# A retention layer into a gated product on one core: where block 1's first product stands, and which engine converts the weights

## The chip, the cores and the metric

The kernel runs on one core of a Trainium2 chip. The metric is the device time of one execution in microseconds. Before the change three runs gave 781.29, 781.69 and 781.89 us, median 781.69.

Engines by the profile's names: PE multiplies matrices (PEld is its load of the stationary operand), DVE is the vector engine, ACT the scalar engine, POOL is GpSimd, and SP's queue (SPq) issues nearly all loads. Times inside the execution are counted from the first instruction.

## The reference, cut to what matters

For each of 4 batches and 8 heads a recurrence runs over 768 steps, and its output, 3072 rows of 512, goes through two matrix products with a sigmoid gate between them.

```
state = gamma * state + outer(k[t], v[t]);   y[t] = scale * q[t] @ state      # head_dim 64
x = y as (4*768, 8*64) = (3072, 512)
h = x @ w_in                    # w_in  512 x 2048
g = h * sigmoid(1.702 * h)
out = g @ w_out                 # w_out 2048 x 512
```

w_in and w_out reach the kernel as 64-bit floats (8 bytes for each weight), and the kernel turns them into 32-bit floats on the chip.

## The kernel before, in words

**Blocks and chunks.** The 3072 rows are six blocks of 512 rows, and a block is four chunks of 128 steps. One chunk j of the recurrence is three steps: `turn(j)` transposes q and k (on PE for chunks 0 to 7, L194, evacuated by ACT, L195; on DVE later, L197) and makes the decayed k on POOL (`kd`, L201); `attend(j)` multiplies k by q on PE (`pa`, L210) and masks it with two DVE multiplications (`at`, L213); `finish(j)` adds the state's part (L223) and the chunk's own part (L227) into `py`, DVE scales that into X (L230), and PE makes the state's update `pu` (L237), which POOL (L244) and DVE (L246, or L242 in the first chunk of a batch) add to the state.

**The two products of a block.** Block 0 takes plain products: `up0(f)` makes the f-th of 16 tiles of h, 128 rows by 512, with four matmuls (L260); ACT takes the sigmoid (L252) and DVE multiplies it in (L253) into G. `down0(f)` adds tile f's part of the output with four matmuls (L272) into four accumulators in PSUM. Both need only the converted weights. Blocks 1 to 5 take `up(d)` and `down(m)`, which make seven products of half size in place of eight (L312, L363). They need sums of the weights, which `sums_w1` and `sums_w2` make on POOL (L281 to L284, L288 to L291), and sums of X and G.

**The weights.** They come in 32 pieces of 512 KB, each a tile of 128 by 512 weights as pairs of 32-bit words (`lo`, `hi`); pieces 0 to 15 are w_in and 16 to 31 w_out. `fetch` loads a piece into one of three raw buffers, which lie in W2's slots 4 to 6. `narrow` converts one piece with eight operations that follow on each other, through two sets of three scratch tiles: ACT takes the magnitude of `hi` (L171); POOL clamps it (L172); DVE shifts it (L173), puts the sign back (L174) and takes the exponent out (L175); ACT converts and scales `lo` (L176); POOL multiplies it by the exponent (L177); DVE adds the two into W1 or W2 (L180). Then the next piece is fetched. Tile f of h needs pieces up to f + 1 at most; `down0(f)` needs piece 16 + f.

**What sets the order.** PE runs in the order that the code is written in. The orders of DVE, ACT, POOL and of SP's queue are made by a scheduler from the same program. Every engine takes its instructions strictly in its order. The code's order is: chunks 0 to 3 with two pieces converted in each; `up0` of block 0, one piece with each tile; `down0` of block 0, one piece with each f, with chunks 4 to 7 and `sums_w1` between them; then blocks 1 to 5, each `up`, then `down` with the next block's chunks between.

The tiles of h go through four PSUM buffers (two tags of two), which are also the four accumulators of `down0`: PE can be four tiles of h ahead of DVE's multiplication.

Of the kernel before, what the change touches and what calls it, by code (L numbers as in the profile page):

```python
# [9 lines left out]
F32 = mybir.dt.float32  # L10
# [18 lines left out]
def kernel(  # L29
# [25 lines left out]


    nc = tc.nc
    pe, act, dve, pool, sp = nc.tensor, nc.scalar, nc.vector, nc.gpsimd, nc.sync
# [32 lines left out]
    G = const.tile([P, NP, 4, TH], F32, name="G")  # L91
    rowd = const.tile([P, HP, P], F32, name="rowd")
    cold = const.tile([P, 2 * H + HP], F32, name="cold")
# [6 lines left out]

    def load(j):

# [8 lines left out]
        if j < 2 * CB:  # L111
            plain("q", q, "q_sq", 2)
            plain("kn", k, "k_sq", 2)
        else:
            for name, src in (("q", q), ("k", k)):
                t = two.tile([P, HP, P // C4, C4], F32, name=name + "_sq")
                for r0 in range(0, P, C4):
                    d0 = r0 % D
                    for hp in range(HP):
                        sp.dma_start(t[r0:r0 + C4, hp],  # L120
                                     src[b, 2 * hp + r0 // D, rows, d0:d0 + C4].rearrange("(s p) d -> p s d", p=C4))
                QKV[name, j] = t
            if c < NC - 1:
                plain("kn", k, "kn", 1)
        plain("v", v, "v", 2)
# [4 lines left out]
    stage = W2[:, 4:7].rearrange("p s n e -> p (s n e)")  # L130
    NRAW, NTMP = 3, 2
    RAWS = [stage[:, 1024 * i:1024 * (i + 1)].bitcast(U32).rearrange("p (n two) -> p n two", two=2)
            for i in range(NRAW)]
    TMPS = [[stage[:, 1024 * NRAW + 512 * (3 * i + t):1024 * NRAW + 512 * (3 * i + t + 1)] for t in range(3)]
            for i in range(NTMP)]

    PIECES = []
    for p in range(NP):
        for h in range(2):
            dst = W1[:, p, 0:4:3] if h == 0 else W1[:, p, 1:3]  # L140
            PIECES.append((dst.rearrange("p ab c f -> p c ab f"), w1v[:, 2 * h:2 * h + 2, 2 * p * P:2 * (p + 1) * P]))
    for p in range(NP):
        for ab in range(2):
            PIECES.append((W2[:, 0:4:3, p] if ab == 0 else W2[:, 1:3, p], w2v[:, 2 * p + ab]))
    N1 = 2 * NP
# [12 lines left out]
    def narrow(n=1):  # L158


        for _ in range(n):
            i = narrowed[0]
            if i == len(PIECES):
                return
            narrowed[0] = i + 1
            w, x = PIECES[i][0], RAWS[i % NRAW]
            lo, hi = x[:, :, 0], x[:, :, 1]
            m, e, r = TMPS[i % NTMP]
            mu, eu = m.bitcast(U32), e.bitcast(U32)

            act.activation(m, hi.bitcast(F32), AF.Abs, scale=2.0 ** 16)  # L171
            pool.tensor_scalar(m, m, F64_MOST * 2.0 ** 16, F64_LEAST * 2.0 ** 16, op0=ALU.min, op1=ALU.max)  # L172
            dve.tensor_scalar(mu, mu, 3, None, op0=ALU.logical_shift_left)  # L173
            dve.scalar_tensor_tensor(mu, hi, 0x80000000, mu, op0=ALU.bitwise_and, op1=ALU.bitwise_or)  # L174
            dve.tensor_scalar(eu, mu, 0xFF800000, None, op0=ALU.bitwise_and)  # L175
            act.activation(r, lo, AF.Copy, scale=2.0 ** -52)  # L176
            pool.tensor_mul(r, r, e)  # L177
            shape = "p (c ab f) -> p c ab f" if i < N1 else "p (s e) -> p s e"
            sizes = dict(c=2, ab=2) if i < N1 else dict(s=2)
            dve.tensor_add(w, m.rearrange(shape, **sizes), r.rearrange(shape, **sizes))  # L180
            fetch()


    QT, KT, KD, AT = {}, {}, {}, {}

    def turn(j):

        for name, store in (("q", QT), ("k", KT)):
            t = one.tile([P, HP, P], F32, name=name + "T")
            if j < 2 * CB:  # L190
# [8 lines left out]
        if j % NC < NC - 1:  # L199
            KD[j] = one.tile([P, H, D], F32, name="kd")  # L200
            pool.tensor_mul(KD[j], QKV.pop(("kn", j)), cold[:, H:2 * H, None].to_broadcast([P, H, D]))  # L201
        if CB <= j < NCH and (j % CB < 2 or j < 2 * CB - 1):
            load(j + (2 if j >= 2 * CB else 1))

    def attend(j):
        p = ps_a.tile([P, 2, HP, P], F32, name="pa")
        for hp in range(HP):
            for i in range(2):
                r = slice(i * D, (i + 1) * D)
                pe.matmul(p[:, i, hp, :], KT[j][r, hp, :], QT[j][r, hp, :], start=True, stop=True)  # L210
        AT[j] = one.tile([P, 2, HP, P], F32, name="at")
        for i in range(2):
# [3 lines left out]
    def finish(j):  # L216
# [12 lines left out]
        half, t0 = divmod(j % CB * P, TH)  # L229
        dve.tensor_mul(X[:, 2 * half:2 * half + 2, :, t0:t0 + P].rearrange("p s c t -> p (s c) t"), y, rowd)  # L230
        if c == NC - 1:
# [17 lines left out]
    def hidden(g, h):  # L249

        s = two.tile([P, 2, TH], F32, name="sg")
        act.activation(s, h, AF.Sigmoid, scale=1.702)  # L252
        dve.tensor_mul(g, h, s)  # L253

    def up0(f):
        p, ab = divmod(f, 2)
        h = ps.tile([P, 2, TH], F32, name="ph", tag="xy"[f % 2])
        for c in range(4):
            w = W1[:, p, (c // 2 if ab == 0 else (3, 2)[c // 2]), c % 2, :]
            pe.matmul(h, w, X[:, c // 2:4:2, c % 2, :], start=(c == 0), stop=(c == 3))  # L260
        hidden(G[:, p, ab:4:2, :], h)

    PO = {}

    def down0(f):
        p, ab = divmod(f, 2)
        for n in range(CB):
# [3 lines left out]
            w = W2[:, 0:4:3, p, :] if ab == 0 else W2[:, 1:3, p, :]  # L271
            pe.matmul(PO[n], G[:, p, 2 * half + ab, t0:t0 + P], w, start=(f == 0), stop=(f == NFF - 1))  # L272
            if f == NFF - 1:
# [130 lines left out]
    load(1)  # L404
    fetch()
    fetch()
    make_identity(nc, ident)
# [11 lines left out]

    for j in range(CB):  # L420
        if j + 2 <= CB:
            load(j + 2)
        turn(j)
        attend(j)
        narrow(1)
        finish(j)
        narrow(1)
    for f in range(NFF):
        up0(f)
        narrow(1)  # L430
    narrow(1)

    def chunks(m):
# [3 lines left out]

    between = chunks(1)
    for f in range(NFF):
        down0(f)  # L440
        narrow(1)
        if between and f >= 2:
            between.pop(0)()
        if f % 4 == 3:
            sums_w1(f // 2 - 1)
    sums_x()
    for m in range(1, NB):
        for d in range(NP // 2):
            up(d)
            if m == 1:  # L450
                sums_w2(2 * d)
            if m + 1 < NB and d < 2:
                load((m + 1) * CB + d)
        between = chunks(m + 1) if m + 1 < NB else []
        for n, unit in enumerate(down(m)):
            unit()
            if between and n % 2:
                between.pop(0)()
# [48 lines left out]
```

## Time and profile before

| what | value |
|---|---|
| median of three runs | 781.69 us |
| the profiled execution's own time, and its span | 782.11 us, 780.3 us |
| PE busy, of the span | 725.1 us, 93% |
| DVE busy | 368.6 us, 47% |
| POOL busy | 206.3 us, 26% |
| ACT busy | 153.4 us, 20% |
| moved by DMA | 46.27 MB, mean 59 GB/s |

The page cuts the span in 40 slices of 19.5 us and gives each engine's busy share in tenths. PE's row reads 4679677499999999999999999999999999999998: the first eight slices, some 156 us, are the only ones in which PE is not nearly always busy. DVE's row begins 3678868761 and POOL's 2776665584 in the same slices. A busy share is an average over a slice. Which wait ended last has to be read from the rows of the chain and the timeline.

### The profile page before, as it was taken

How to read it: one execution, taken by the hardware profiler on the slowest of the kernel's cores; microseconds unless marked ns; L12 is line 12 of the kernel's file. 1: busy time of each engine (PE TensorE's matmuls, PEld its weight loads, DVE VectorE, ACT ScalarE, POOL GpSimd, SP SyncE). 2: the span in 40 equal slices, each digit the busy share in tenths (PEclk: the TensorE clock that was granted, in tenths of full speed). 3: DMA queues.
4: the chain of work that ended last, by engine and by line, in shares of the span. 5: the costliest groups of instructions: out<-in, count | busy, mean ns of one | idle time of the engine just before them, and what ended most of it. 6: DMA issues, size and time to landing. Idle time of an engine off the chain costs nothing.

```text
span 780.3 us, 9581 instructions
## 1 busy us (share of the span) xinstructions
PE 725.1 (93%) x3648; PEld 572.4 (73%) x3648; DVE 368.6 (47%) x547; ACT 153.4 (20%) x253; POOL 206.3 (26%) x195
## 2 busy tenths in 40 slices
PE   4679677499999999999999999999999999999998
PEld 3454222155568888888888888888888888888886
DVE  3678868761144336334436434445334364244251
ACT  3233334310103310013300023300033200033100
POOL 2776665584140004020014220012300022200030
PEclk9879878699999999999999999999999999999999
DMA  8634323312241003340022331022430030100001
GB/s 202 185 113 149 134 108 109 133 29 55 45 109 23 1 15 77 56 99 14 1 54 53 84 60 22 1 50 55 85 71 1 0 69 13 42 1 1 1 13 41
DMA packets 142253, 46.27 MB, mean 59 GB/s; under 512 B 129920, under 2 KB 135552, under 8 KB 142208
## 3 DMA queue, kind: packets, MB, share of 16 engines
q1 hardware_dynamic: 135504, 39.10, 21.5%
q10 hardware_dynamic: 6704, 6.57, 2.5%
q8 instruction: 29, 0.48, 0.2%
q14 instruction: 16, 0.13, 0.1%
HBM read 39.33 MB, written 6.29 MB: 58 GB/s over the span
## 4 chain that ended last, share of the span: by engine, by line
PE 77%; DVE 11%; POOL 7%; issue 3%; DMA 1%; SPq 0%; ACT 0%; POOLq 0%; DVEq 0%
PE pd L363 30%; PE px L312 18%; PE py L312 13%; PE po L272 5%; PE py L227 4%; POOL W L177 3%; PE pu L237 3%; PE pa L210 3%; DVE W L174 3%; DVE W L180 2%; DVE W L173 2%; PE py L223 2%; DVE W L175 1%; POOL W L172 1%; DMA W<-in_moe_w_in_dram 1%
## 5 line engine op out<-in xcount | busy, mean ns | idle before, releaser
L363 PE MATMUL pd<-W,G 128*128 128x256 f32 x1120 | 250.3, 381 | 0.4 <-DVE G L303 0.3
L363 PEld LDWEIGHTS pd<-W,G 128*128 128x128 f32 x1120 | 210.1, 190 | 30.8 <-DVE G L303 1.2
L312 PE MATMUL px<-X,W 128*128 128x256 f32 x640 | 148.7, 379 | 0.0
L312 PEld LDWEIGHTS px<-X,W 128*128 128x128 f32 x640 | 121.6, 190 | 17.0 <-issue 0.5
L312 PE MATMUL py<-X,W 128*128 128x256 f32 x480 | 113.4, 379 | 0.0
L312 PEld LDWEIGHTS py<-X,W 128*128 128x128 f32 x480 | 91.2, 190 | 12.4
L201 POOL TENSOR_TENSOR kd<-kn_in,cold 128x512 f32<-128x512 f32 x20 | 22.2, 1110 | 294.3 <-PE pu L237 200.4
L260 PE MATMUL ph<-X,W 128*128 128x512 f32 x128 | 65.8, 671 | 16.9 <-DVE G L253 16.9
L272 PE MATMUL po<-W,G 128*128 128x512 f32 x128 | 61.8, 628 | 10.4 <-DVE G L253 10.4
L213 DVE TENSOR_TENSOR at<-pa,mask 128x512 f32<-128x512 f32 x48 | 30.9, 685 | 83.6 <-PE pa L210 83.5
L260 PEld LDWEIGHTS ph<-X,W 128*128 128x128 f32 x128 | 26.6, 214 | 55.4 <-issue 30.9
L304 POOL TENSOR_TENSOR G<-G 128x512 f32<-128x512 f32 x20 | 29.0, 1449 | 111.5 <-DVE G L303 107.0
L272 PEld LDWEIGHTS po<-W,G 128*128 128x128 f32 x128 | 24.3, 199 | 39.2 <-issue 24.9
L252 ACT ACTIVATE sg<-G 128x512 f32<-128x512 f32 x60 | 37.8, 631 | 64.0 <-DVE G L322 38.3
L177 POOL TENSOR_TENSOR W<-W 128x512 f32<-128x512 f32 x32 | 43.5, 1360 | 25.8 <-DVE W L175 25.8
L253 DVE TENSOR_TENSOR G<-G,sg 128x512 f32<-128x512 f32 x60 | 41.3, 689 | 17.4 <-ACT sg L252 17.4
L227 PE MATMUL py<-at,v_in 128*64 128x128 f32 x384 | 32.2, 303 | 11.3 <-DVE at L213 11.3
L180 DVE TENSOR_TENSOR W<-W 128x512 f32<-128x512 f32 x32 | 30.3, 946 | 26.4 <-POOL W L177 26.1
L171 ACT ACTIVATE W<-W 128x512 f32<-128x512 f32 x32 | 21.6, 675 | 87.7 <-DVE W L180 79.1
L227 PEld LDWEIGHTS py<-at,v_in 128*64 128x64 f32 x384 | 24.5, 150 | 17.1 <-DVE at L213 13.7
L210 PEld LDWEIGHTS pa<-qT,kT 64*128 64x128 f32 x384 | 24.1, 193 | 15.4 <-issue 7.3
L322 DVE TENSOR_TENSOR G<-py,p 128x512 f32<-128x512 f32 x20 | 13.8, 692 | 44.4 <-PE py L312 44.4
(66 smaller groups left out, 620.5 us busy)
## 6 DMA issues: line engine op xcount, KB each, us to landing
W<-in_moe_w_in_dram SPq DMA_DIRECT2D x16, 512.0 KB, 4.0
W<-in_moe_w_out_dram SPq DMA_DIRECT2D x16, 512.0 KB, 3.2
v_in<-in_v_dram SPq DMA_DIRECT2D x24, 256.0 KB, 3.3
out_dram<-o ACTq DMA_DIRECT2D x24, 256.0 KB, 2.3
kn_in<-in_k_dram SPq DMA_DIRECT2D x21, 256.0 KB, 3.7
q_sq<-in_q_dram SPq DMA_DIRECT2D x256, 16.0 KB, 1.8
k_sq<-in_k_dram SPq DMA_DIRECT2D x256, 16.0 KB, 1.7
q_in<-in_q_dram SPq DMA_DIRECT2D x8, 256.0 KB, 5.2
```

Source lines behind the costliest of these rows:

```text
L177: pool.tensor_mul(r, r, e)
L180: dve.tensor_add(w, m.rearrange(shape, **sizes), r.rearrange(shape, **sizes))
L210: pe.matmul(p[:, i, hp, :], KT[j][r, hp, :], QT[j][r, hp, :], start=True, stop=True)
L213: dve.tensor_mul(AT[j][:, i], p[:, i], mask[:, i])
L227: pe.matmul(y[i * D:(i + 1) * D, hp, :], vn[:, 2 * hp + i, :], a[:, i, hp, :], start=(not c and hp == 0), stop=(hp == HP - 1), skip_group_ ...
L252: act.activation(s, h, AF.Sigmoid, scale=1.702)
L253: dve.tensor_mul(g, h, s)
L260: pe.matmul(h, w, X[:, c // 2:4:2, c % 2, :], start=(c == 0), stop=(c == 3))
L272: pe.matmul(PO[n], G[:, p, 2 * half + ab, t0:t0 + P], w, start=(f == 0), stop=(f == NFF - 1))
L304: pool.tensor_sub(g[1], g[1], g[0])
L312: pe.matmul(acc[:, u, :], W1[:, 2 * d + u, sa, c, :], X[:, sb, c, :], start=(start and u == 0 and c == 0), stop=(stop and c == 1), skip_gr ...
L363: pe.matmul(p0[:, n, :], G[:, p, sa, n * P:(n + 1) * P], W2[:, sb, p, :], start=(new and p == 0 and n == 0), stop=(last and p == NP - 1), ...
```

## The change

Three things move together.

**The order.** Chunks 4 to 7 run between the tiles of `up0` of block 0 (one step after each tile from the third on), block 1 then takes its first product in the plain form too (`up0(1, f)`, 16 tiles in place of four `up(d)`), and only then comes `down0` of block 0. In the first four chunks `turn(j + 1)` now stands between `attend(j)` and `finish(j)`. `sums_w2` stands in `down0`, `sums_w1` in block 1's `down`.

**The conversion.** After ACT's magnitude, all six operations on a piece are DVE's: clamp, shift, sign, exponent, product, sum. They are done in place, in the raw buffer and in the piece's own place in W1 or W2, so that no scratch tiles are left. ACT converts `lo` no more and POOL does nothing for a piece. There are four raw buffers in place of three, in slots 4 and 5 of W2.

**Where things lie.** Block 0's G goes to slots 4 to 6 of W1, slots 4 to 6 of X and a small tile, since block 1's takes the old place; its DVE multiplications are cut in two halves of 256. Block 1's X lies in slot 6 of W2. For chunks 0 to 7 the transposed q, k, the decayed k and the masked product lie in G, in two sets.

```diff
-    NRAW, NTMP = 3, 2
+    NRAW = 4
...
             act.activation(m, hi.bitcast(F32), AF.Abs, scale=2.0 ** 16)
-            pool.tensor_scalar(m, m, F64_MOST * 2.0 ** 16, F64_LEAST * 2.0 ** 16, op0=ALU.min, op1=ALU.max)
+            dve.tensor_scalar(m, m, F64_MOST * 2.0 ** 16, F64_LEAST * 2.0 ** 16, op0=ALU.min, op1=ALU.max)
             dve.tensor_scalar(mu, mu, 3, None, op0=ALU.logical_shift_left)
-            dve.scalar_tensor_tensor(mu, hi, 0x80000000, mu, op0=ALU.bitwise_and, op1=ALU.bitwise_or)
-            dve.tensor_scalar(eu, mu, 0xFF800000, None, op0=ALU.bitwise_and)
-            act.activation(r, lo, AF.Copy, scale=2.0 ** -52)
-            pool.tensor_mul(r, r, e)
...
-            dve.tensor_add(w, m.rearrange(shape, **sizes), r.rearrange(shape, **sizes))
+            dve.scalar_tensor_tensor(hi, hi, 0x80000000, mu, op0=ALU.bitwise_and, op1=ALU.bitwise_or)
+            dve.tensor_scalar(mu, hi, 0xFF800000, None, op0=ALU.bitwise_and)
+            r = lo.bitcast(F32)
+            dve.scalar_tensor_tensor(r, lo, 2.0 ** -52, m, op0=ALU.mult, op1=ALU.mult)
...
+                dve.tensor_add(w, xf[:, :, :, :, 1], xf[:, :, :, :, 0])
...
+        for g, h, s in [(g, h, s)] if not isinstance(g, list) else [(g[i], h[:, i], s[:, i]) for i in range(2)]:
+            dve.tensor_mul(g, h, s)
...
+    def g0(p, s):
+        if s < 3:
+            return W1[:, p, 4 + s].rearrange("p c f -> p (c f)")
+        return X[:, 4 + p // 2, p % 2] if p < 6 else G0[:, p % 2]
...
+    turn(0)
     for j in range(CB):
-        if j + 2 <= CB:
-            load(j + 2)
-        turn(j)
         attend(j)
         narrow(1)
+        turn(j + 1)
         finish(j)
         narrow(1)
+    between = chunks(1)[1:]
     for f in range(NFF):
-        up0(f)
+        up0(0, f)
+        if f < NP or f % 4 == 3:
+            narrow(1)
+        if between and f >= 2:
+            between.pop(0)()
+    for f in range(NFF):
+        up0(1, f)
         narrow(1)
-    narrow(1)
...
     for f in range(NFF):
         down0(f)
-        narrow(1)
-        if between and f >= 2:
-            between.pop(0)()
         if f % 4 == 3:
-            sums_w1(f // 2 - 1)
-    sums_x()
+            sums_w2(f // 2 - 1)
```

How the orders move, at the two places on which the prediction rests. First PE, from block 0's first product on, before (`ph` is a tile of h, `po` block 0's output, `pt`, `pa`, `py`, `pu` the steps of a chunk):

```order
L260 MATMUL ph<-X,W_72 128x512 x64
L272 MATMUL po<-W_73,G 128x512 x12
L194 MATMUL pt<-ident,q_in 128x128 x4
L194 MATMUL pt<-ident,kn_in 128x128 x4
L272 MATMUL po<-W_73,G 128x512 x4
L210 MATMUL pa<-qT,kT 128x128 x8
L272 MATMUL po<-W_73,G 128x512 x4
```

And now, from chunk 7's masked product on (X1 lies in W2, hence `ph<-W_73`; block 0's G lies in W1 and X):

```order
L231 MATMUL pa<-G 128x128 x8
L291 MATMUL ph<-X,W_72 128x512 x4
L244 MATMUL py<-G,state_82 128x128 x4
L248 MATMUL py<-G,v_in 64x128 x8
L261 MATMUL pu<-v_in,G 128x128 x4
L291 MATMUL ph<-X,W_72 128x512 x12
L291 MATMUL ph<-W_73,W_72 128x512 x64
L303 MATMUL po<-W_73,W_72 128x512 x6
```

The chunks now stand among the tiles of `ph`, and sixteen more tiles stand ahead of the first `po`.

Second DVE, while pieces of w_out are converted. Before (L253 is the multiplication into G):

```order
L174 SCALAR_TENSOR_TENSOR W_73<-W_73 128x512
L175 TENSOR_SCALAR W_73<-W_73 128x512
L173 TENSOR_SCALAR W_73<-W_73 128x512
L174 SCALAR_TENSOR_TENSOR W_73<-W_73 128x512
L253 TENSOR_TENSOR G<-ph,sg 128x2x256
L180 TENSOR_TENSOR W_73<-W_73 128x2x256
L175 TENSOR_SCALAR W_73<-W_73 128x512
L180 TENSOR_TENSOR W_73<-W_73 128x2x256
```

And now, in block 1's first product (L178 clamp, L179 shift, L180 sign, L181 exponent, L183 product, L190 sum, L278 the multiplication into G):

```order
L180 SCALAR_TENSOR_TENSOR W_73<-W_73 128x512 [waits DMAHW1_49,DVE_49]
L278 TENSOR_TENSOR W_72<-ph,sg 128x256 [waits Activation_49]
L278 TENSOR_TENSOR g_76<-ph,sg 128x256
L181 TENSOR_SCALAR W_73<-W_73 128x2x256 [waits DVE_49]
L178 TENSOR_SCALAR W_73<-W_73 128x2x256
L183 SCALAR_TENSOR_TENSOR W_73<-W_73 128x512 [waits DVE_49]
L179 TENSOR_SCALAR W_73<-W_73 128x2x256 [waits DVE_49]
L190 TENSOR_TENSOR W_73<-W_73 128x2x256 [waits DVE_49]
L180 SCALAR_TENSOR_TENSOR W_73<-W_73 128x512 [waits DMAHW4_49,DVE_49]
L278 TENSOR_TENSOR G<-ph,sg 128x2x256 [waits Activation_49]
```

Two pieces are woven into each other, so that an operation seldom stands right behind the one that it waits for, and none of DVE's rows waits for POOL. In DVE's whole order the last piece's sum stands ahead of the multiplication of tile 6 of block 1: 32 halves and 6 whole multiplications stand ahead of it, and tiles 6 to 15 behind.

More of the change, by code (lines that the diff above doesn't have):

```diff
@@ L91 @@
     G = const.tile([P, NP, 4, TH], F32, name="G")
+    G0 = one.tile([P, 2, TH], F32, name="g0", tag="s1")
+    X1 = W2[:, 6].rearrange("p (s c) t -> p s c t", s=4)
     rowd = const.tile([P, HP, P], F32, name="rowd")
@@ L111, in load @@
         if j < 2 * CB:
-            plain("q", q, "q_sq", 2)
-            plain("kn", k, "k_sq", 2)
+            if "q" in what:
+                plain("q", q, "q_sq", 2)
+                plain("kn", k, "k_sq", 2)
         else:
@@ L124, in load @@
                 plain("kn", k, "kn", 1)
-        plain("v", v, "v", 2)
+        if "v" in what:
+            plain("v", v, "v", 2)
     w1v = moe_w_in.bitcast(U32).rearrange("(c p) (f two) -> p c f two", p=P, two=2)
     w2v = moe_w_out.bitcast(U32).rearrange("(f p) (e two) -> p f e two", p=P, two=2)
-    stage = W2[:, 4:7].rearrange("p s n e -> p (s n e)")
-    NRAW, NTMP = 3, 2
[L132 to L135, printed above, removed]
+    NRAW = 4
+    RAWS = [W2[:, 4 + i // 2, i % 2 * 4:i % 2 * 4 + 4].rearrange("p n e -> p (n e)").bitcast(U32)
+            .rearrange("p (n two) -> p n two", two=2) for i in range(NRAW)]
     PIECES = []
@@ L186, in turn @@
     def turn(j):
         for name, store in (("q", QT), ("k", KT)):
[L189 removed]
+            t = home(j, name + "T")
             if j < 2 * CB:
@@ L404 @@
     load(1)
-    fetch()
-    fetch()
+    for _ in range(NRAW - 1):
+        fetch()
     make_identity(nc, ident)
```

86 lines of the change are left out of this document (53 added, 33 removed).

## The prediction

> **What bounds the kernel now.** I read the totals of four stages first. They are cut where the chain of waits changes hands. A row gives the stage, its length, and busy time (instructions) of PE, PEld, DVE, ACT and POOL, then the granted clock, DMA share and GB/s.
>
> ```profile
> 9.00:54.00 45.00, 28.76 (x201) 23.44 (x201) 28.53 (x45) 15.36 (x26) 27.48 (x27) 0.86 0.67 178
> 54.00:173.00 119.00, 91.75 (x209) 39.27 (x208) 90.26 (x120) 38.94 (x66) 79.25 (x73) 0.85 0.32 108
> 173.00:276.00 103.00, 102.31 (x489) 72.66 (x489) 34.73 (x55) 19.79 (x33) 22.56 (x21) 1.00 0.21 44
> 276.00:780.00 504.00, 500.11 (x2745) 435.55 (x2744) 212.90 (x319) 78.03 (x128) 74.15 (x68) 1.00 0.18 38
> ```
>
> From 173 us on PE is busy 602 of 607 us: there only less PE work helps. Before 173 us no engine is full, DVE and POOL come nearest, and PE's share is inflated by waiting matmuls. Who hands to whom stands in the chain that ended last (start, length, what):
>
> ```profile
> 157.20 1.28 POOL W L177
> 171.18 1.74 DVE W L180
> 176.35 3.44 PE po L272 x8
> 227.85 1.73 PE px L312 x8
> 276.19 6.91 PE pd L363 x32
> ```
>
> Up to 171 us it goes through the conversion, POOL and DVE in turn. From 176 us it is PE alone. The 171.18 row is the last piece: the conversion ends at 172.9 us, and until then PE lacks work, since `down0` needs w_out. Block 1's first product stands from 227.85 to 276.19, 48.3 us, where PE is full anyway.
>
> **The change, part by part.** *PE's account.* `up(1)` goes (48.3 us). `up0(1)` comes: 16 tiles of four matmuls. One such group of four (the x8 of the 176.35 row, two records for each) takes 3.44 us, so 55.0 us. PE has 6.7 us more to do in all. The gain can come only from filling the time before the conversion's end: chunks 4 to 7 and `up0(1)` need no w_out, and 17 + 55 us of PE work move in there.
>
> *One piece's price on DVE.* First the four kinds that the trace has, as min/median/max, and then with their means over all 32:
>
> ```profile
> L173 DVE TENSOR_SCALAR W<-W x32: 410/416/1501, 11.0 to 161.3; 128x512 uint32<-128x512 uint32 x32
> L174 DVE SCALAR_TENSOR_TENSOR W<-W x32: 677/716/1645, 11.5 to 162.9; 128x512 uint32<-128x512 uint32 x32
> L175 DVE TENSOR_SCALAR W<-W x32: 411/424/1482, 12.2 to 166.1; 128x512 uint32<-128x512 uint32 x32
> L180 DVE TENSOR_TENSOR W<-W x32: 675/693/1750, 14.1 to 171.2; 128x512 f32<-128x512 f32 x32
> ...
> L174 DVE SCALAR_TENSOR_TENSOR W<-W 128x512 uint32<-128x512 uint32 x32 | 31.1, 971 | 0.7
> L180 DVE TENSOR_TENSOR W<-W 128x512 f32<-128x512 f32 x32 | 30.3, 946 | 26.4 <-POOL W L177 26.1
> L173 DVE TENSOR_SCALAR W<-W 128x512 uint32<-128x512 uint32 x32 | 21.6, 676 | 14.6 <-POOL W L172 14.6
> L175 DVE TENSOR_SCALAR W<-W 128x512 uint32<-128x512 uint32 x32 | 19.9, 622 | 0.4
> ```
>
> The four take 102.9 us where their medians make 32 x 2.25 = 72 us: 31 us are stretch. The timeline shows where it comes from:
>
> ```profile
> 11.02 0.43 DVE L173 TENSOR_SCALAR W<-W 128x512 uint32<-128x512 uint32 x1 [7.14 <-POOL W L172]
> 11.48 0.69 DVE L174 SCALAR_TENSOR_TENSOR W<-W 128x512 uint32<-128x512 uint32 x1
> 12.20 0.43 DVE L175 TENSOR_SCALAR W<-W 128x512 uint32<-128x512 uint32 x1
> ...
> 47.45 1.27 POOL L177 TENSOR_TENSOR W<-W 128x512 f32<-128x512 f32 x1
> ...
> 47.52 1.48 DVE L173 TENSOR_SCALAR W<-W 128x512 uint32<-128x512 uint32 x1 [0.51 <-POOL W L172]
> 49.03 0.69 DVE L174 SCALAR_TENSOR_TENSOR W<-W 128x512 uint32<-128x512 uint32 x1
> 49.64 0.68 DVE L180 TENSOR_TENSOR W<-W 128x512 f32<-128x512 f32 x1
> 50.24 0.42 DVE L175 TENSOR_SCALAR W<-W 128x512 uint32<-128x512 uint32 x1
> 50.70 1.29 DVE L213 TENSOR_TENSOR at<-pa,mask 128x512 f32<-128x512 f32 x2
> ```
>
> L173 at 47.52 starts 0.07 us behind a POOL operation and ends at 49.00, 0.28 us after that one's end: it takes 1.06 us more than at 11.02. The Trainium skill, "SBUF — State Buffer", section "Who interferes with whom", says that a DVE operation with two SBUF inputs, or in the two-port mode, and a GpSimd operation shut each other out for a whole instruction; this row agrees, and by that rule the stretch leaves together with POOL's operations.
>
> An operation right behind the one that it needs starts 0.46 us after a tensor_scalar begins and 0.72 us after the longer kind (the rows at 11.02 to 12.20). With other work between, the longer kind starts every 0.60 to 0.61 us (49.03, 49.64, 50.24); for a tensor_scalar I take 0.34 by the same 0.12 less, an estimate. A piece is now three tensor_scalar (clamp, shift, exponent) and three of the longer kind (sign, product, sum): from 3 x 0.34 + 3 x 0.60 = 2.82 us to 3 x 0.46 + 3 x 0.72 = 3.54 us, for 32 pieces 90 to 113 us. The new order weaves two pieces nearly everywhere but not always, so I take the middle, 101 us.
>
> What the trace lacks is a tensor_scalar that reads every second word (the exponent, L181 now). L174 reads `hi` at that stride at its kind's usual 0.69 us, so the stride alone does no harm there. The cost lies between 0.42 and 0.69 us; I take the lower, and the upper adds 32 x 0.27 = 8.6 us. The Trainium skill, "VectorE: DVE Perf Modes", section "What auto-detection actually checks", names no stride as a condition of the two-port mode at 32 bits, only SBUF on both sides and the outer dimensions' sizes; by it the lower end holds, and no run here shows it yet. Writing `hi` and the product back at that stride is also unseen; both ends go into the range.
>
> *DVE's other work before the last piece's end.* Rows of the groups:
>
> ```profile
> L213 DVE TENSOR_TENSOR at<-pa,mask 128x512 f32<-128x512 f32 x48 | 30.9, 685 | 83.6 <-PE pa L210 83.5
> L230 DVE TENSOR_TENSOR X<-py,rowd 128x512 f32<-128x512 f32 x24 | 16.5, 689 | 19.9 <-PE py L227 19.9
> L246 DVE TENSOR_TENSOR state<-state,pu 64x256 f32<-64x256 f32 x32 | 13.3, 415 | 6.2 <-PE pu L237 5.7
> L253 DVE TENSOR_TENSOR G<-ph,sg 128x512 f32<-128x512 f32 x16 | 10.9, 680 | 0.2 <-ACT sg L252 0.2
> L201 POOL TENSOR_TENSOR kd<-kn_in,cold 128x512 f32<-128x512 f32 x20 | 22.2, 1110 | 294.3 <-PE pu L237 200.4
> L244 POOL TENSOR_TENSOR state<-state,cold 64x256 f32<-64x256 f32 x32 | 20.8, 652 | 1.2
> ```
>
> Eight chunks: 16 masks at 0.64 (half of the 50.70 row's 1.29), 8 scalings at 0.69, 14 state operations at 0.42, together 21.7 us. Block 0's multiplications in halves are a new size; between half of 0.68 and the 0.42 of 256 elements in L246 I take 0.40, so 32 make 12.8 us. Six whole ones of block 1 at 0.61: 3.7 us. POOL keeps 8 x 1.11 + 10 x 0.65 = 15.4 us in this stretch. Before, 31 us of stretch stood against 107 us of POOL work (27.48 + 79.25), 0.29 for each; that leaves 4.5 us. DVE will also wait for PE in the chunks. L230 and L246 show 19.9 and 5.7 us of that over 24 chunks, so 8.5 us for eight; with two block transposes I allow 12 us, an estimate.
>
> *The sum.* DVE begins at 10.4 us, where POOL clamps the first piece now:
>
> ```profile
> 10.37 0.62 POOL W L172
> ```
>
> 10.4 + 101 + 21.7 + 12.8 + 3.7 + 4.5 + 12 = 166 us for the end of the conversion, in place of 172.9. Then DVE multiplies tile 6 of block 1 (0.7 us), which frees the PSUM buffer for tile 10; tiles 10 to 15 take PE 6 x 3.44 = 20.6 us, to 187.4; `down0` takes 55.0 us more, and 0.5 us for two hand-overs: `down(1)` starts at 243 us in place of 276.2. That is 33 us. Behind it the same work stands as before. `sums_w1` now runs on POOL at the end of `down0` and into `down(1)`, under PE work of 50 us; POOL has 22.6 of 103 us busy in that stretch today. It is free of charge as long as it ends before `up(2)`, and if that cover failed each microsecond past it would count in full.
>
> The four raw buffers and the loads I cost at nothing. The early stage moves 178 GB/s at a share of 0.67, and a piece in flight has three pieces' time, some 9 us, to land. Chunks 4 to 7 bring twelve loads forward in SP's queue, and the small loads of chunk 8 now stand between the fetches, up to nine of them:
>
> ```profile
> L120 SPq DMA_DIRECT2D q_sq<-in_q_dram x256: 311/430/1789, 194.8 to 637.4; - x128
> ```
>
> Nine take 3.9 us of the queue, under a piece's 3.2 us and the multiplication beside it (0.6 us) only just; most gaps hold five. Three pieces ahead cover that. If the cover fails, DVE idles and the end moves by as much. 782.1 - 33.2 = 748.9 us by the profiled execution, which is 0.4 us above the median of the runs: I predict **749 us**.
>
> **The rivals.** *PE sets the pace* (faster still). PE's rows for a chunk, in this order a transposition, the masked product, the state's part, the chunk's own part and the update:
>
> ```profile
> 179.78 0.88 PE pt L194 x8
> 184.09 1.09 PE pa L210 x16
> 188.82 0.89 PE py L223 x8
> 189.71 1.02 PE py L227 x16
> 204.42 1.09 PE pu L237 x8
> ```
>
> The eleven steps between the tiles are 3 transpositions, 4 masked, 3 states, 4 own, 3 updates: 17 us. With 110 us of tiles, 127 us. `up0` can start when the last X is there, before at 54.7 us:
>
> ```profile
> 54.05 0.69 DVE L230 TENSOR_TENSOR X<-py,rowd 128x512 f32<-128x512 f32 x1 [1.23 <-PE py L227]
> ```
>
> Now from the first mask, some 15 us, DVE has 5.3 pieces (16.7 us), eight masks, four scalings and six state operations (10.4 us) and some 9 us of stretch and waits ahead of it: 51 us. 51 + 127 = 178, `down(1)` at 233.5, 739 us. For it: the weave is dense, and DVE could take 2.82 us for a piece. Against it: the two engines wait on each other in fixed orders.
>
> *DVE in full dependence* (a smaller gain). At 3.54 us a piece (+12) and with twice the idle time (+12): 749 + 24 = 773 us. The strided exponent at 0.69 would give 749 + 8.6 = 758. For it: every conversion operation waits for the one before it in its piece.
>
> *The stretch isn't POOL's* (slower). Then six operations on DVE keep today's means: 3 x about 0.66 + 3 x 0.96 = 4.86 us a piece, 155.5 us in place of 101 + 4.5, so 50 us later: 799 us. It decides from 33 / 32 = 1.04 us more a piece, that is from 4.2 us on. DMA writing to the raw buffers, or the in-place strided writes, could do that. Against it: the medians lie at the unstretched values, and the stretched row ends just behind the POOL operation.
>
> *It doesn't overlap*: loads queue behind each other in SP's order, pieces come late by a third of the gap, and the gain is gone; 776 to 785 us. Against it: a DMA share of 0.32 between 54 and 173 us.
>
> **How the numbers follow.** The forecast, 743 to 760 us: 0.55. PE's pace, 737 to 743: 0.15. Full dependence, 760 to 776: 0.20. No overlap: 0.04. Slower by stretch: 0.06. The range 738 to 770 leaves out a part of the last three and little of the second, some 0.2. A measurement of this kernel tells 0.2% (1.6 us) from no change. Faster 0.92, the same 0.02, slower 0.06.
>
> **What would show it.** Right: in the profile after, `pd` begins near 243 us; DVE's six operations average below 0.45 and 0.72 us; DVE is over 85% busy from 50 to 166 us and the chain goes through it there, then through PE from some 166 us on; PE is full from there. Wrong: conversion operations at 1 us without POOL work beside them; DVE idle behind a piece's landing; a stop of PE between `down0` and `up(2)` behind POOL's sums.

## The result, and the profile after

The changed kernel takes 735.76 us (median of four runs, 735.23 to 736.34); the kernel before took 781.79 us beside it (781.29 to 782.37). The ratio is 0.941, 95% interval 0.9395 to 0.9427: 46 us less, where 33 us were forecast. The time lies 2 us below the predicted range. The profiled execution took 735.37 us with a span of 733.6 us.

The chain of waits of the changed kernel (start, length, what), at the places that answer to those shown of before:

```profile
45.25 11.30 PE ph L291 x24
...
108.93 65.23 PE ph L291 x152
174.16 54.93 PE po L303 x128
229.10 6.91 PE pd L394 x32
```

Up to 45.25 us the chain goes through loads, DVE and PE in turn; from the first tile of h on it is PE alone. Block 1's second product (`pd`) begins at 229.10 in place of 276.19 us, 47.1 us earlier, and the spans differ by 46.7 us. So all of the gain lies ahead of that point. The stages of the changed kernel (window, length, busy time of PE, PEld, DVE, ACT and POOL, then the granted clock, DMA share, GB/s):

```profile
9.00:45.00 36.00, 26.40 (x216) 21.61 (x217) 32.55 (x57) 12.70 (x20) 9.57 (x10) 0.93 0.91 215
45.00:100.00 55.00, 55.00 (x248) 29.70 (x247) 53.96 (x116) 17.82 (x30) 6.27 (x7) 0.98 0.66 176
100.00:150.00 50.00, 50.00 (x156) 23.77 (x155) 49.91 (x99) 13.72 (x23) 10.91 (x8) 1.00 0.48 131
150.00:175.00 25.00, 25.00 (x60) 11.13 (x59) 6.38 (x11) 4.78 (x8) 4.97 (x5) 1.00 0.12 19
```

Two engines are full at once between 45 and 150 us. A busy share doesn't tell which of them sets the end. The end of the conversion in DVE's timeline does (L190 is the last piece's sum, L278 the multiplication into G):

```profile
149.04 1.13 DVE L190 TENSOR_TENSOR W<-W 128x512 f32<-128x512 f32 x1
150.09 2.09 DVE L278 TENSOR_TENSOR G<-ph,sg 128x512 f32<-128x512 f32 x3
154.23 0.69 DVE L278 TENSOR_TENSOR G<-ph,sg 128x512 f32<-128x512 f32 x1 [2.04 <-ACT sg L276]
157.66 0.69 DVE L278 TENSOR_TENSOR G<-ph,sg 128x512 f32<-128x512 f32 x1 [2.74 <-ACT sg L276]
```

The conversion ends at 150.1 us. Block 1's tile 10 is the first that needs a buffer which DVE frees behind it, and it starts 6 x 3.43 us before 174.16, at 153.6 us. DVE is there 3 us before it is needed, and from 154 us on it waits for PE's tiles, which reach it through ACT's sigmoid (L276). The six operations of a piece, seven of their nine groups by shape, with busy time and mean ns of one:

```profile
L178 DVE TENSOR_SCALAR W<-W 128x512 f32<-128x512 f32 x32 | 15.6, 494 | 6.4 <-ACT W L177 6.4
L181 DVE TENSOR_SCALAR W<-W 128x512 uint32<-128x512 uint32 x32 | 15.5, 485 | 0.2
L179 DVE TENSOR_SCALAR W<-W 128x512 uint32<-128x512 uint32 x32 | 14.1, 443 | 0.1
L183 DVE SCALAR_TENSOR_TENSOR W<-W,W 128x512 f32<-128x512 uint32 x16 | 12.8, 800 | 0.1
L187 DVE TENSOR_TENSOR W<-W 128x512 f32<-128x512 f32 x16 | 12.5, 780 | 0.0
L190 DVE TENSOR_TENSOR W<-W 128x512 f32<-128x512 f32 x16 | 11.5, 719 | 0.0
L180 DVE SCALAR_TENSOR_TENSOR W<-W 128x512 uint32<-128x512 uint32 x16 | 11.1, 692 | 0.0
```

They average 0.44 to 0.49 us and 0.69 to 0.80 us, where before they took 0.62 to 0.68 and 0.95 to 0.97 us. The strided exponent (L181) costs what a tensor_scalar costs.

### The profile page after: what moved, and what is told of

Same layout as the page of the kernel before. It is cut to its first block, busy times and chain, and to the rows that moved or that the text cites. A ratio compares the mean times of both kernels' runs of the same rounds, so it can differ in the third digit from the quotient of the medians.

```text
span 733.6 us, 9285 instructions
## 1 busy us (share of the span) xinstructions
PE 712.6 (97%) x3552; PEld 547.0 (75%) x3552; DVE 359.8 (49%) x611; ACT 127.7 (17%) x209; POOL 136.0 (19%) x127
## 4 chain that ended last, share of the span: by engine, by line
PE 93%; DVE 4%; DMA 1%; issue 0%; ACT 0%; SPq 0%; DVEq 0%
PE pd L394 32%; PE ph L291 15%; PE px L343 15%; PE py L343 11%; PE po L303 7%; PE pa L231 3%; PE py L248 3%; PE pu L261 3%; PE py L244 2%; DMA W<-in_moe_w_in_dram 1%; DVE G L333 1%; PE pt L215 1%; DVE W L187 1%; DVE G L334 0%; DVE W L183 0%
## 5 line engine op out<-in xcount | busy, mean ns | idle before, releaser
L343 PE MATMUL px<-X,W 128*128 128x256 f32 x512 | 119.0, 379 | 0.0
L343 PEld LDWEIGHTS px<-X,W 128*128 128x128 f32 x512 | 97.3, 190 | 13.2
L343 PE MATMUL py<-X,W 128*128 128x256 f32 x384 | 90.7, 379 | 0.0
L343 PEld LDWEIGHTS py<-X,W 128*128 128x128 f32 x384 | 73.0, 190 | 9.9
L291 PE MATMUL ph<-W,W 128*128 128x512 f32 x128 | 55.1, 592 | 0.0
L291 PEld LDWEIGHTS ph<-W,W 128*128 128x128 f32 x128 | 24.3, 190 | 30.6 <-issue 30.4
L303 PE MATMUL po<-W,W 128*128 128x512 f32 x96 | 42.5, 592 | 0.0
L278 DVE TENSOR_TENSOR G<-G,sg 128x512 f32<-128x512 f32 x48 | 33.1, 689 | 14.1 <-ACT sg L276 14.1
L276 ACT ACTIVATE sg<-G 128x512 f32<-128x512 f32 x48 | 30.3, 631 | 51.3 <-DVE G L353 30.7
L303 PEld LDWEIGHTS po<-W,W 128*128 128x128 f32 x96 | 18.2, 190 | 23.0 <-issue 23.0
L177 ACT ACTIVATE W<-W 128x512 f32<-128x512 f32 x32 | 21.8, 685 | 54.4 <-DMA W<-in_moe_w_out_dram 30.6
L268 POOL TENSOR_TENSOR state<-state,cold 64x256 f32<-64x256 f32 x32 | 21.2, 663 | 53.1 <-DVE state L270 27.6
L276 ACT ACTIVATE sg<-ph 128x512 f32<-128x512 f32 x32 | 19.0, 595 | 51.3 <-PE ph L291 43.3
```

The lines of the kernel that those rows point to most:

```text
L268: pool.tensor_mul(new[r, :, r], old[r, :, r], cold[r, 2 * H:, None].to_broadcast([D, HP, D]))
L291: pe.matmul(h, w, x[:, c // 2:4:2, c % 2, :], start=(c == 0), stop=(c == 3))
L303: pe.matmul(PO[n], g0(p, 2 * half + ab)[:, t0:t0 + P], w, start=(f == 0), stop=(f == NFF - 1))
L343: pe.matmul(acc[:, u, :], W1[:, 2 * d + u, sa, c, :], X[:, sb, c, :], start=(start and u == 0 and c == 0), stop=(stop and c == 1), skip_gr ...
```

## The experiments

Once the profile after was read, the theory became that PE paces the changed kernel from its first tile on and DVE has slack behind that tile; the rival was that DVE, full from 45 to 150 us, is the pace or nearly so.

### One part alone: the order, or the conversion

The changed order, with the conversion shared out again over ACT, POOL and DVE, through three raw buffers:

```diff
-            dve.tensor_scalar(m, m, F64_MOST * 2.0 ** 16, ...)
+            pool.tensor_scalar(m, m, F64_MOST * 2.0 ** 16, ...)
...
-            dve.scalar_tensor_tensor(r, lo, 2.0 ** -52, m, op0=ALU.mult, op1=ALU.mult)
+            act.activation(r, lo, AF.Copy, scale=2.0 ** -52)
+            pool.tensor_mul(r, r, m)
```

> The changed order, but each piece is converted as before by three engines: clamp and product on POOL, `lo` scaled by ACT into one of two scratch tiles, three raw buffers; VectorE keeps four operations. Theory (the conversion on VectorE alone is needed, since POOL's operations stretch VectorE's and each hand-over costs a wait): VectorE's four operations average again above 0.55 us (tensor_scalar) and 0.85 us (the longer kind), the conversion ends near 170 us instead of 150, PE waits in block 1's first product, and the time is 750 to 762 us. Rival (the order alone brings the gain): within 4 us of the changed kernel's 736 us, PE without a stop from 46 us on.

Measured 762.27 us (758.67 to 764.73), ratio 0.9746 (0.9713 to 0.9779), at the upper edge of the theory's 750 to 762 us. Its chain, and two groups of its conversion:

```profile
167.69 36.30 PE ph L294 x80
203.99 54.93 PE po L306 x128
258.92 6.91 PE pd L397 x32
...
L180 POOL TENSOR_SCALAR W<-W 128x512 f32<-128x512 f32 x32 | 23.4, 733 | 20.5 <-ACT W L179 20.2
L182 DVE SCALAR_TENSOR_TENSOR W<-W,W 128x512 uint32<-128x512 uint32 x16 | 17.5, 1092 | 0.9
```

The conversion's last sum ends at 167.0 us, and ten tiles of block 1 (80 records, eight for each) are still to do: this is the forecast's mechanism, with PE held by DVE's buffers until the conversion is over, and `pd` at 259. The sign (L182) averages 1092 ns in these 16, and 0.69 us in the changed kernel, where POOL does nothing for a piece. Shift and exponent average 535 and 525 ns, just below the 0.55 us that the theory had named.

The order of before, with the conversion on DVE alone and four pieces in flight:

> The order of before (block 0's second product ahead of block 1's first, which stays in seven half-size products), with only the conversion changed: VectorE alone, in place, four raw buffers. Theory (from some 46 us on PE is the limit as soon as VectorE converts at 3.2 us a piece, whatever the order): w_out's piece 16 + f is there before the f-th step of the second product, PE has no stop, and since block 1's first product takes 48.3 us in place of 55.0, down(1) starts at 47 to 50 + 55 + 55 + 17 + 48.3 = 222 to 226 us and the time is 727 to 733 us, below the changed kernel. Rival (the order is what fills PE, as its second product must wait for w_out): PE stops between 100 and 150 us, time 745 to 765 us.

Measured 747.54 us (746.99 to 748.24), ratio 0.9559 (0.9542 to 0.9576). The rival was right; the theory's 727 to 733 us missed. The stage from 100 to 150 us, and its chain:

```profile
100.00:150.00 50.00, 42.44 (x140) 19.87 (x138) 49.87 (x91) 12.52 (x21) 26.60 (x10) 0.90 0.47 143
...
119.05 0.61 DVE G L257
119.70 9.96 PE po L276 x18
```

DVE is full and PE stops for 7.6 us of the 50. Until 119 us the chain goes through the conversion. All that PE has before `down0` here is block 0's 16 tiles, which end behind the w_in pieces. Taken singly the conversion brings 34.5 us and the order (with the overlapped first chunks) 20, together 46: they overlap, since each of them shortens the same stretch in which PE lacks work.

The same with the first chunks overlapped as in the change (`turn(j + 1)` ahead of `finish(j)`):

> As the one before (order of blocks as before, conversion by VectorE), and the first four chunks overlapped as in the change (turn of the next chunk ahead of finish, transposed tiles in two sets in G). Theory: the first product starts at 45 us as in the changed kernel, PE then has 175 us to down(1) at 221 us: 724 to 728 us, the best of all. Rival (order needed): 742 to 762 us.

Measured 747.7 us (747.07 to 749.45): the same as without, and the theory's 724 to 728 us missed. PE waits 7.2 us for DVE's multiplications in `down0`. The first tile starts only 1.1 us earlier here (48.52 for 49.59), and that does not reach the end.

### Without the plain first product of block 1

If chunks 4 to 7 among block 0's tiles are cover enough, the 6.7 us that `up0(1)` costs PE can be saved: conversion on DVE, overlap, chunks moved, then `down0`, and block 1 keeps its product of half size.

```diff
     for f in range(NFF):
-        down0(f)
+        up0(f)
         narrow(1)
         if between and f >= 2:
             between.pop(0)()
+    for f in range(NFF):
+        down0(f)
+        narrow(1)
```

> The conversion by VectorE and the overlapped first chunks as in the change, chunks 4 to 7 among the tiles of block 0's first product as in the change, but then block 0's second product at once, and block 1's first product in seven half-size products after it as before (block 0's X lies in slot 6 of W2). Theory (what made the conversion alone stop PE is that the 17 us of chunks 4 to 7 stood behind w_out's pieces; with them ahead PE has 72 us of work from 45 us on, and piece 16 + f is there at 117 + 3.4 f us): no stop of PE from 46 us on, down(1) at 45 + 72 + 55 + 48.3 = 221 us, 725 to 730 us, below the changed kernel by the 6.7 us that the plain form of block 1's product costs. Rival (block 1's whole first product is needed ahead of w_out): PE stops in block 0's second product, 737 to 748 us.

Measured 753.46 us (753.14 to 753.75), ratio 0.9643 (0.9626 to 0.9659): a miss. PE stops for 7.0 us between 134 and 144 us, where `po` waits for multiplications that stand behind pieces in DVE's order, and before that for 6.5 us between 65 and 102 us, behind the chunks' masks. Then block 0's X in another place, and 18 pieces called ahead of `down0`, so that the multiplications would come sooner:

> As e5 (chunks 4 to 7 among block 0's tiles, block 0's second product next, block 1's first product in half sizes after it), but without the two things that stood behind PE's stop in e5: block 0's X lies in slot 4 of W1, so that most of POOL's sums of w_in's weights can start only when block 0's first product is done, and 18 pieces in place of 24 are called for ahead of the second product, so that fewer stand ahead of the tiles' multiplications. Theory (PE has enough work ahead of w_out with chunks 4 to 7 alone, 72 us from 45 us on, once VectorE keeps 3.2 us a piece): no stop of PE over 1 us, down(1) at 45 + 74 + 55 + 48.3 = 222 us, 727 to 731 us, below the changed kernel. Rival (block 1's plain first product is needed as cover): PE stops in the second product, 736 us or more.

Measured 751.81 us (751.32 to 751.92), ratio 0.962 (0.9604 to 0.9636): the rival again, and 1.7 us below the one before. The stage from 125 to 150 us, and DVE's and POOL's timelines in it:

```profile
125.00:150.00 25.00, 10.94 (x17) 4.26 (x18) 25.00 (x26) 3.20 (x6) 19.96 (x13) 0.66 0.26 73
...
127.81 1.48 DVE L178 TENSOR_SCALAR W<-W 128x512 uint32<-128x512 uint32 x1
129.21 1.49 DVE L176 TENSOR_SCALAR W<-W 128x512 uint32<-128x512 uint32 x1
130.62 1.75 DVE L180 SCALAR_TENSOR_TENSOR W<-W 128x512 f32<-128x512 uint32 x1
132.29 0.68 DVE L274 TENSOR_TENSOR G<-ph,sg 128x512 f32<-128x512 f32 x1
...
127.57 2.85 POOL L302 TENSOR_TENSOR W<-W 128x512 f32<-128x512 f32 x2
130.38 3.11 POOL L304 TENSOR_TENSOR W<-W 128x512 f32<-128x512 f32 x2
```

POOL makes the sums of the weights that the half-size product needs, and beside them DVE's conversion takes an operation about every 1.4 or 1.7 us in place of 0.34 or 0.60. The multiplications come every 8 to 9 us, and PE, which waits for each, is busy 11 of 25 us. The Trainium skill, "SBUF — State Buffer", section "Who interferes with whom", says that a DVE operation with at most one SBUF input, outside the two-port modes, doesn't contend with GpSimd; the row at 132.29, which reads PSUM and one SBUF tile, agrees: 0.68 us in the midst of the others. So `up0(1)` does two things at once. It is 55 us of PE work that needs no piece of w_out, and it puts off most of POOL's sums until the conversion is over (from 100 to 150 us POOL is busy 10.9 us in the changed kernel, 30.6 us here). Its 6.7 us are the price. No run separates the two.

### Is DVE or PE the pace of the changed kernel?

The clamp left out (so this kernel's conversion isn't the reference's for values outside the 32-bit range; every other part is there):

> The changed kernel without the clamp of the magnitude (one tensor_scalar of 0.42 us for each piece, 32 in all; weights that are zero or beyond a float's range would come out wrong). It leaves that part out, so it is not a full kernel. Theory (PE sets the pace from 46 us on): only the pieces ahead of the first product count, 7 x 0.42 = 2 to 3 us: 732 to 735 us. Rival (VectorE sets the pace to the end of the conversion, as the prediction had it): 32 x 0.36 = 11 us: 723 to 726 us.

Measured 733.27 us (733.09 to 733.65), ratio 0.9379 (0.9365 to 0.9393). Of some 11 us taken off DVE (32 x 0.34), 2.5 us reach the time. PE is the pace. The clamp three times over:

> The changed kernel with the clamp made three times (the second and third change nothing): 64 more tensor_scalar of 0.42 us on VectorE, starting every 0.36 us. Theory (PE sets the pace with 3.5 us to spare on VectorE: the last piece ends at 149.7 us, tile 6 of block 1 is multiplied by 150.4, and PE reaches tile 10 at 153.5): 7 pieces, 5 us, ahead of the first tile count in full; of all 23 us some 3.5 are slack, so VectorE becomes the limit and the time rises by 18 to 20 us to 754 to 757 us. Rival (VectorE has much more slack than that, since its order could be let slip): 5 us, 740 to 742 us.

Measured 741.86 us (741.53 to 744.96), ratio 0.9493 (0.9474 to 0.9511); the theory's 754 to 757 missed, the rival's 740 to 742 held. Its profiled execution is the slowest of the runs, 3.1 us above the median. Two rows of PE's and DVE's timelines:

```profile
49.72 10.57 PE L292 MATMUL ph<-X,W 128*128 128x512 f32 x24 [1.98 <-DVE X L253]
...
176.43 1.13 DVE L191 TENSOR_TENSOR W<-W 128x512 f32<-128x512 f32 x1
```

The conversion ends at 177.6 us, 27 us later than in the changed kernel, and PE still has no stop behind 70 us. I had taken the order as fixed: tile 6 behind the last piece. The scheduler put eleven of block 1's multiplications ahead of the last sum in place of six, so the buffers came free in time. The slack of 3 us is that of one order, and DVE's slack up to `down0` is larger. That corrects the theory in its size, not in its kind.

Thirty products on POOL that nothing uses, one with each piece from the third on, made from the piece converted two before:

```diff
+            pool.tensor_mul(spare, mask[:, 0], mask[:, 1])
```

> The changed kernel with one product of 128 x 512 on POOL for each piece from the third on, into a tile that nothing reads; nothing of VectorE waits for it (30 operations of some 1.3 us). Theory (POOL's operations shut VectorE's out): VectorE's conversion operations go from 0.42 to 0.49 and 0.69 to 0.80 us on average to above 0.52 and 0.85 us, the conversion ends some 11 us later, of which 3 us are slack: 741 to 749 us. Rival (the stretch of before came from the hand-overs or from DMA, not from POOL's work beside VectorE): averages as in the changed kernel within 0.03 us, 735 to 737 us.

Measured 744.79 us (744.39 to 745.93), ratio 0.9534 (0.952 to 0.9548), in the theory's range. Groups, then PE's two longest stops among block 0's tiles, and the end of the conversion on DVE and on PE:

```profile
L181 POOL TENSOR_TENSOR spare<-W 128x512 f32<-128x512 f32 x30 | 36.8, 1227 | 70.9 <-DVE W L191 38.8 <-DVE W L194 31.9
L182 DVE TENSOR_SCALAR W<-W 128x512 f32<-128x512 f32 x32 | 26.2, 823 | 6.0 <-ACT W L177 6.0
...
64.19 0.43 PE L252 MATMUL py<-G,v_in 128*64 128x128 f32 x2 [1.89 <-DVE G L238]
...
96.95 0.43 PE L252 MATMUL py<-G,v_in 128*64 128x128 f32 x2 [1.57 <-DVE G L238]
...
162.01 2.69 DVE L282 TENSOR_TENSOR G<-ph,sg 128x512 f32<-128x512 f32 x4
162.74 20.87 PE L295 MATMUL ph<-W,W 128*128 128x512 f32 x48 [1.08 <-DVE G L282]
```

36.8 us of POOL work make the conversion end 11.9 us later (162.0 for 150.1), 0.32 us for each; the prediction had taken 0.29 from before. Most of it falls on the clamp, 823 in place of 494 ns. The longer kind kept its mean of 0.73 us over all 96, where the theory had named above 0.85; only the three tensor_scalar grew, from 0.47 to 0.60 us. Here DVE is late for tile 10 of block 1, and PE stops 1.08 us for it: the mechanism of the forecast appears as soon as the conversion ends at 162 us in this order. That stop is short because PE had already lost time: it stopped for 4.7 us between 62 and 98 us behind the masks that DVE makes for the chunks (L238).

### What stands ahead of the first tile

The first chunks one after the other, then three raw buffers:

```diff
-    turn(0)
     for j in range(CB):
+        turn(j)
         attend(j)
         narrow(1)
-        turn(j + 1)
         finish(j)
```

> The changed kernel with the first four chunks one after the other as before (turn, attend, finish; chunk 4's turn among the tiles). Theory (PE sets the pace from its first tile on, and the first tile's time passes one to one into the end): the first product starts some 3 to 8 us later than 45.2 us and the time is that much above 736 us: 738 to 744 us. Rival (the overlap is worth nothing, as VectorE's pieces fill the same time): 735 to 737 us.

> The changed kernel with three raw buffers in place of four. Theory (the loads have slack: a piece lands in 4 us and two pieces' time is 6 us): 735 to 738 us, VectorE's idle time before the first product at most 2 us more. Rival (four in flight are needed): VectorE waits for ACT's magnitude behind the loads, 740 to 752 us.

Measured 739.79 us (738.3 to 741.35), ratio 0.9468 (0.945 to 0.9486), and 738.21 us (736.66 to 740.48), ratio 0.945 (0.9428 to 0.9472). The first lies in the theory's range, the second 0.2 us above its 735 to 738. Without the overlap the first tile starts at 49.10 us and the span is 4.3 us longer. The profiled executions side by side (us; the start of the first tile in PE's timeline, of the first `po` in the chain, and the span, against the changed kernel's 45.04, 174.16 and 733.6):

| kernel | first tile | first `po` | span |
|---|---|---|---|
| no clamp | -1.5 | -2.0 | -2.0 |
| three raw buffers | +1.3 | +2.3 | +2.2 |
| no overlap | +4.1 | +4.2 | +4.3 |
| clamp three times | +4.7 | +9.6 | +9.6 |
| idle POOL work | +0.9 | +9.5 | +9.0 |

What comes late ahead of the first tile stays in the time to the end. The last two add stops of PE behind it, most of them behind the masks of the chunks.

That points to a better kernel: of the pieces converted ahead of the first tile, tile f needs only those up to f + 1. So one piece in each of the first four chunks in place of two, and one with every tile of block 0; then the same with two pieces in all.

```diff
         finish(j)
-        narrow(1)
     between = chunks(1)[1:]
     for f in range(NFF):
         up0(0, f)
-        if f < NP or f % 4 == 3:
-            narrow(1)
+        narrow(1)
```

> The changed kernel, but with one piece converted in each of the first four chunks in place of two, and a piece with every tile of block 0. In VectorE's order 5 pieces' sums, and 24.0 us of work by the start-to-start times (0.34 and 0.60 us an operation), now stand ahead of the fourth X, in place of 6 pieces and 26.8 us. Theory (TensorE paces from its first tile on, VectorE has slack behind it, so what stands ahead of that tile counts one for one): first tile 2.8 us earlier, near 42.5 us, no stop behind it, 731.5 to 734.5 us. Rival (with fewer pieces in hand VectorE becomes the pace among block 0's tiles): TensorE stops between 50 and 110 us for a piece or a multiplication, 735 to 742 us.

> As the one before, but only two pieces are converted in the first four chunks; the scheduler still draws five pieces' sums ahead of the fourth X (24.0 us of work ahead of it, as there), and w_in's sixteenth piece comes 3 us of work later (69.9 in place of 67.0 us; 65.1 in the changed kernel). Theory: the same as the one before, 731.5 to 734.5 us, since the slack behind the first tile covers 3 us more. Rival: VectorE is the pace among block 0's tiles, and this one is slower than the one before by up to 3 us, 735 to 745 us.

Measured 728.27 us (727.77 to 728.77), ratio 0.9318 (0.9305 to 0.9331), and 728.6 us (728.52 to 728.88), ratio 0.9323 (0.9311 to 0.9336). Both are some 7 us faster than the changed kernel, more than the 2.8 us expected and below the theory's range, and alike, as the theory had it. The first of them, PE's timeline ahead of the first tile and then the chain:

```profile
36.10 1.09 PE L248 MATMUL py<-G,v_in 128*64 128x128 f32 x16
37.12 1.16 PE L261 MATMUL pu<-v_in,G 128*128 128x128 f32 x8
39.13 10.57 PE L291 MATMUL ph<-X,W 128*128 128x512 f32 x24 [0.85 <-DVE X L252]
...
102.05 65.24 PE ph L291 x152
167.28 54.93 PE po L303 x128
```

And the changed kernel there, PE's timeline, then DVE's, then three windows:

```profile
40.34 0.69 PE L248 MATMUL py<-G,v_in 128*64 128x128 f32 x2 [2.41 <-DVE G L234]
41.27 1.97 PE L248 MATMUL py<-G,v_in 128*64 128x128 f32 x14 [0.24 <-DVE G L234]
43.17 2.08 PE L261 MATMUL pu<-v_in,G 128*128 128x128 f32 x8
45.04 11.51 PE L291 MATMUL ph<-X,W 128*128 128x512 f32 x24
...
37.43 1.53 DVE L187 TENSOR_TENSOR W<-W 128x512 f32<-128x512 f32 x1
...
38.00:40.00 2.00, 0.00 (x0) 0.00 (x0) 1.97 (x3) 0.38 (x1) 0.41 (x1) 1.00 0.00 0
42.00:44.00 2.00, 2.00 (x14) 1.67 (x11) 1.81 (x5) 1.07 (x2) 0.00 (x0) 0.50 1.28 259
44.00:46.00 2.00, 2.00 (x8) 1.48 (x8) 1.21 (x3) 0.88 (x1) 0.15 (x1) 0.50 1.20 246
```

Of the 6.9 us between the spans, 5.9 lie ahead of the first tile (45.04 against 39.13). The fourth X comes 4.9 us sooner (38.39 for 43.28 in the two timelines of DVE): 2.8 us are the conversion that now stands behind it, and the other 2 us are what stretch and waits differ by (the row at 37.43, 1.53 us in place of 0.69, is one of the stretched operations). Between that X and the first tile lie 1.0 us less, since PE in the changed kernel runs at half the clock there, behind a stop of 2.41 us. The last 0.9 us come from the first 24 matmuls, which take 11.51 in place of 10.57 us for the same reason. That the scheduler put the two masks of the last chunk next to each other in the new kernel, and a conversion operation ahead of the first and between the two in the changed one, may be what ended PE's stop; no run varied that alone.

## Why the prediction was right or wrong

**The bound, and where the gain lies: right.** Nothing from `pd` on changed, and all of the gain came from the stretch in which PE lacked work.

**The conversion's price: right in its sum, by luck in its parts.** I worked out 101 us, the middle between two woven pieces and full dependence, with the stretch by POOL as a term of its own. Counted from each start to the next over DVE's timeline, the operations take 101.3 us, and the stretch lies within that. Against 90 us of dense weave, 22 lengthened operations add some 9.7 us and late starts behind the operation needed some 1.6. So the weave was nearly perfect, and the stretch was twice the 4.5 us allowed. POOL's price of 0.29 was close to the 0.32 measured, but POOL was busy 26.8 us between 9 and 150 us in place of the 15.4 counted, since `sums_w2` starts at 136 us. The strided exponent holds the lower end (median 422 ns). The Trainium skill, "VectorE: DVE Perf Modes", section "What auto-detection actually checks", names no stride as a condition of the two-port mode, and the trace agrees. Chunks and multiplications came to 20.4 and 14.3 us, for 21.7 and 16.5.

**The step that failed: the allowances.** The sum held 12 us for waits and transposes and 4.5 us for stretch. Between 10.6 and 150.1 us DVE waited 2.2 us in all and the transposes took 1.3: 3.5 us in place of 12. This is the largest miss, 8.5 us. Conversion and stretch together took 101.3 in place of 105.5, and chunks and multiplications 3.5 us less than their terms: that is the whole difference between 166 and 150 us. I had taken the waits over from the kernel before, where L230 and L246 wait for PE. In the new order DVE's windows from 45 to 150 us are full: operations of a piece stand where it would have waited.

**What followed from it: the wrong case.** With the end at 166 us DVE sets the pace and `pd` starts at 243. With 150 us it doesn't, and the rival "PE sets the pace" decides. Its mechanism is what happened: its 127 us from the first tile to `po` measured 128.9, and `down0` 54.9 for 55.0. Its start was mis-sized by the same allowance: 51 us for the first tile, of which some 9 us were stretch and waits, where 45.25 was measured. At 45.25 + 127 + 55 us it would have given 733 us by the profiled execution. I put the rival at 0.15 because "the two engines wait on each other in fixed orders". The full windows from 45 to 150 us contradict that, and the experiment with thirty products on POOL shows how near it was: with DVE 12 us later, PE does wait.

**The signs.** `pd` began at 229 in place of some 243 us, and the chain went through PE from 45 us on, where I had looked for DVE until 166. DVE was over 85% busy there, as I had said; a full engine did not mean the pace. Clamp and exponent averaged 0.49 us, above the 0.45 named, and product and sum 0.75 to 0.76, above 0.72: the stretch again.

**The other rivals.** Full dependence, stretch that isn't POOL's, and loads that come too late did not occur. Nine small loads at 3.9 us do not fit under 3.2 and 0.6 us, as the prediction had it, but nothing came of it: DVE waited 5.69 us for the first piece, 0.75 for the second and for none behind. Four raw buffers were costed at nothing; three cost 2.5 us. `sums_w1` under `down(1)` is free, as worked out: PE has no stop between 229 and 300 us.

**What the prediction didn't look for.** It counted DVE's work ahead of the first tile as given, and so missed that one piece less there, 2.8 us of work, would come with 7 us.

## What to carry to other kernels

Waits of an engine are not a property of its instructions: where a change gives it work that is always ready, waits of the old profile must not be added to the new sum, and the rival in which it has slack deserves more than the 0.15 that I gave it. If two engines are both full, find out which is late for the other at one place (here a PSUM buffer: DVE ready at 150.7, PE at 153.6 us), and then ask what stands ahead of the pace-setter's first work; here that counted in full to the end. A first product in a dearer form can pay if it needs nothing that is late and puts off work that disturbs.

## What the hardware showed that I had not expected

**A dense DVE can hold POOL off for long.** It goes both ways. In the last half-size kernel, while DVE converts without a gap behind 146 us, one of POOL's sums takes 10.43 us, where others of its kind take 1.3 to 1.7:

```profile
151.12 10.43 POOL L310 TENSOR_TENSOR W<-W 128x512 f32<-128x512 f32 x1 [5.05 <-DVE W L187]
```

In the stretch ahead of it, up to 146 us, POOL's operations follow on each other almost without a gap, and there each of DVE's conversion operations lasts until 0.3 to 0.6 us behind the end of one of them. Which of the two is held seems to hang on whose next instruction is ready; no run settled it.

**The clock falls behind a short stop of PE.** After 2.41 us without a matmul the granted clock was 0.50 from 42 to 46 us, and eight update matmuls took 2.08 us in place of 1.16. The Trainium skill, "TensorE: Matmul & The Clock Gate", section "HAM oscillation — how this bites in real kernels", puts the gap that does this above some 3.4 us; here the drop came behind a shorter one. The length of a stop does not settle it in these runs. In the kernel without overlap stops of 1.83 and 1.55 us left the clock at 1.00. In the kernel with thirty products on POOL one of 1.89 us did so too, but one of 1.57 us was followed by a clock of 0.50:

```profile
64.00:66.00 2.00, 1.06 (x14) 0.82 (x15) 2.00 (x4) 0.00 (x0) 1.62 (x2) 1.00 0.75 261
...
98.00:100.00 2.00, 2.00 (x15) 1.67 (x12) 2.00 (x5) 0.35 (x1) 0.16 (x1) 0.50 0.65 207
```

What else decides is open.
